# Attention in 64x64 tiles with an instruction order planned at build time

## The chip, the cores and the metric

The kernel runs on one core of one Trainium2 chip. The metric is the device time of one execution in microseconds. An execution counts as slow when it is more than 1.5% above the fastest of the same kernel; ratios compare fast ones only. The span of a profile (first to last instruction) is some 1.7 us shorter than the time of the same execution.

## The reference

```python
# q, k, v: 8 batches x 12 heads x 448 tokens x 64
scores = (q @ k.T) / sqrt(64)
attn   = maximum(scores, 0) ** 2 / 448
x      = attn @ v                                  # to 8 x 448 x 768
h      = maximum(x.T @ w_tok1, 0) @ w_tok2         # token mixing, 448 -> 256 -> 448
u      = x + h.T
out    = u + maximum(u @ w_ch1, 0) @ w_ch2         # channel mixing, 768 -> 1536 -> 768
```

Inputs and output are float32; the kernel computes in bf16 and accumulates in float32.

## The kernel before

It takes two heads a step, 48 steps. 448 keys are cut into three blocks of 128 and a remainder of 64; the remainders of the two heads share one block whose other halves are zero (`kz`, `vz`).

```python
def transposes(s):            # 16 transposes, 128x64 tiles, into one bank
    blocks = [(c * QP, QP, q_raw[:, :, c, :]) for c in range(QC)]            # 4 of 112
    blocks += [(KO + c * 128, 128, k_raw[:, :, c, :]) for c in range(KB)]    # 3 of 128
    blocks.append((KO + KM, 128, kz...))                                     # remainder
    for at, n, src in blocks:
        for h in range(2):
            nc.tensor.matmul(ps[64 * h : 64 * (h + 1), at : at + n], lhsT=src[:, h, :],
                             rhs=ident[:n, :n], is_transpose=True, ...)
    nc.vector.tensor_copy(sb, ps[:, : KO + KM + 128])

def scores(s, blocks):        # 64x128 tiles: one row half for each head
    for c in blocks:
        ps = ps_att.tile([128, 2, 512], FP32, tag="att", name="sc_ps")       # two banks
        for e in range(2):
            nc.tensor.matmul(ps[:, e, :S], lhsT=sb[h, KO + c * 128 : ...], rhs=sb[h, :S], ...)
    # ACT: at = relu(ps), both banks at once; DVE later: sq = at * at

def values(s):                # 128x64 tiles, then values_rest with a full 128x128 tile
    ...
# ... cut: x_back, token1, token2, channel1, channel2

for s in range(NS + 4):       # a fixed order, written by hand
    scores(s, (0, 1)); load_pair(s + PRE); transposes(s + 1)
    values(s - 1); scores(s, (2,)); values_rest(s - 1)
    square(); fill(0.25)      # a quarter of the step's share of channel work
    scores_rest(s); x_back(s - 2); fill(0.25); square()
    token2(...); fill(0.25); token1(...); fill(0.25)
```

Conditions and arguments are cut here. PSUM is split for good: two tiles of two banks for scores, one bank for values, three for all else. Channel work of a batch can start only when its six pairs have gone through token mixing.

## Time and profile before

| | before |
|---|---|
| median time | 413.28 us (4 runs, 411.98 to 415.08) |
| profiled span | 411.6 us |
| TensorE busy | 388.3 us, 94% |
| ACT, DVE busy | 51%, 53% |
| first channel matmul | 58.2 us |
| idle stretches of TensorE after that | hardly any until the end |

The page's busy share says which engine to look at; it does not say what a step costs, because TensorE's matmuls overlap. The distance from the start of one block to the start of the next does. The timeline of TensorE shows, in brackets, how long it stood idle and what ended that; these two rows are from the start of the kernel before:

```profile
27.76 1.86 PE L290 MATMUL t_ps<-x_sb,wt 128*128 128x256 bf16 x8 [4.38 <-DVE x_sb L280]
...
40.40 1.03 PE L290 MATMUL t_ps<-x_sb,wt 128*128 128x256 bf16 x8 [2.24 <-DVE x_sb L280]
```

Token 1 stands in the order ahead of score groups that could have run, so all of TensorE waits for one copy. The first row's eight matmuls take 1.86 us where the second's take 1.03: after 4.38 us of idling the granted clock is 0.50 there (stretch from 27.7 to 29.6 us).

### The profile page before, as it was taken

How to read it: one execution, taken by the hardware profiler on the slowest of the kernel's cores; microseconds unless marked ns; L12 is line 12 of the kernel's file. 1: busy time of each engine (PE TensorE's matmuls, PEld its weight loads, DVE VectorE, ACT ScalarE, POOL GpSimd, SP SyncE). 2: the span in 40 equal slices, each digit the busy share in tenths (PEclk: the TensorE clock that was granted, in tenths of full speed). 3: DMA queues.
4: the chain of work that ended last, by engine and by line, in shares of the span. 5: the costliest groups of instructions: out<-in, count | busy, mean ns of one | idle time of the engine just before them, and what ended most of it. 6: DMA issues, size and time to landing. Idle time of an engine off the chain costs nothing.

```text
span 411.6 us, 7596 instructions
## 1 busy us (share of the span) xinstructions
PE 388.3 (94%) x3033; PEld 205.4 (50%) x3033; DVE 216.2 (53%) x414; ACT 209.5 (51%) x313; POOL 130.8 (32%) x196
## 2 busy tenths in 40 slices
PE   5856799999999999999999999999999999999995
PEld 2323345555445555555445555555545555555562
DVE  2667774466465566365455665356444755432021
ACT  2745676743674446753575347654566237611400
POOL 8995456244243333243223424235222000000000
PEclk9778999999999999999999999999999999999999
DMA  7999999459946999469955989569953434113323
GB/s 75 119 145 203 187 180 196 57 80 126 167 50 69 137 137 143 45 93 134 134 70 56 146 131 147 57 75 134 149 70 47 93 92 92 24 47 99 60 62 93
DMA packets 101572, 43.44 MB, mean 106 GB/s; under 512 B 83424, under 2 KB 97952, under 8 KB 101536
## 3 DMA queue, kind: packets, MB, share of 16 engines
q0 software_dynamic: 54432, 21.70, 50.2%
q1 hardware_dynamic: 47104, 21.25, 25.3%
q8 instruction: 24, 0.39, 0.4%
q14 instruction: 12, 0.10, 0.1%
HBM read 43.38 MB, written 11.01 MB: 132 GB/s over the span
## 4 chain that ended last, share of the span: by engine, by line
PE 85%; DVE 7%; POOL 4%; issue 1%; DMA 1%; ACT 0%; DVEq 0%; ACTq 0%; POOLq 0%
PE m_ps L345 26%; PE m_ps L363 26%; PE sc_ps L195 8%; PE acc_ps L226 6%; PE qkT_ps L163 6%; PE t_ps L290 5%; PE h_ps L308 3%; PE acc_ps L240 3%; DVE sq L185 3%; PE sr_ps L209 2%; DVE uT_sb L316 1%; DMA wt_nat<-in_moe_w_tok_dram 1%; DVE xT L248 1%; POOL k_raw L86 1%; POOL v_raw L94 1%
## 5 line engine op out<-in xcount | busy, mean ns | idle before, releaser
L179 ACT ACTIVATE at<-sc_ps 128x896 bf16<-128x896 f32 x144 | 122.5, 922 | 60.3 <-PE sc_ps L195 59.9
L345 PE MATMUL m_ps<-uT_sb,wc 128*128 128x448 bf16 x576 | 120.3, 352 | 0.6 <-DVE uT_sb L316 0.5
L363 PE MATMUL m_ps<-wc,r_sb 128*128 128x384 bf16 x672 | 116.7, 326 | 0.0
L185 DVE TENSOR_TENSOR sq<-at 128x896 bf16<-128x896 bf16 x192 | 97.7, 559 | 0.1
L94 POOL DMA_DIRECT2D v_raw<-in_v_dram x48 | 34.5, 719 | 170.1 <-PE sc_ps L195 159.3
L363 PEld LDWEIGHTS <-r_sb 128*128 128x128 bf16 x672 | 65.6, 98 | 44.3 <-issue 0.6
L352 ACT ACTIVATE r_sb<-m_ps 128x448 bf16<-128x448 f32 x96 | 52.1, 543 | 65.9 <-PE m_ps L345 65.9
L345 PEld LDWEIGHTS <-wc 128*128 128x128 bf16 x576 | 56.2, 98 | 49.7 <-issue 1.4
L173 DVE COPY qkT<-qkT_ps 128x960 bf16<-128x960 bf16 x48 | 31.5, 656 | 85.6 <-PE qkT_ps L163 85.6
L371 DVE TENSOR_TENSOR out_sb<-m_ps,u_sb 128x384 f32<-128x384 f32 x56 | 31.1, 555 | 71.4 <-PE m_ps L363 69.2
L195 PE MATMUL sc_ps<-qkT 64*128 64x448 bf16 x288 | 45.6, 365 | 2.5 <-ACT at L179 1.3
L248 DVE TENSOR_SCALAR xT<-acc_ps 128x448 bf16<-128x448 f32 x48 | 29.9, 624 | 29.7 <-PE acc_ps L240 29.7
L226 PE MATMUL acc_ps<-sq,v_raw 128*64 128x448 bf16 x288 | 36.7, 363 | 0.0
L82 POOL DMA_DIRECT2D q_raw<-in_q_dram x48 | 33.0, 688 | 10.8 <-DMA wc<-in_moe_w_ch_dram 9.8
L86 POOL DMA_DIRECT2D k_raw<-in_k_dram x48 | 35.2, 732 | 1.7 <-DMA wc<-in_moe_w_ch_dram 1.7
L179 ACT ACTIVATE at<-sr_ps 128x448 bf16<-128x448 f32 x48 | 26.2, 545 | 16.8 <-PE sr_ps L209 16.8
L290 PE MATMUL t_ps<-x_sb,wt 128*128 128x256 bf16 x192 | 25.7, 278 | 9.0 <-DVE x_sb L280 9.0
L298 ACT ACTIVATE r_sb<-t_ps 128x512 bf16<-128x512 f32 x24 | 14.3, 597 | 38.4 <-PE t_ps L290 38.4
L195 PEld LDWEIGHTS <-qkT 64*128 64x128 bf16 x288 | 10.8, 94 | 37.2 <-issue 35.8
L316 DVE TENSOR_TENSOR uT_sb<-h_ps,xT 128x448 bf16<-128x448 f32 x48 | 27.6, 615 | 2.0 <-PE h_ps L308 2.0
L290 PEld LDWEIGHTS <-wt 128*128 128x128 bf16 x192 | 19.0, 99 | 15.0 <-issue 5.1
L163 PEld LDWEIGHTS <-q_raw 112*64 112x64 bf16 x384 | 12.3, 113 | 22.4 <-issue 18.0
(36 smaller groups left out, 209.0 us busy)
## 6 DMA issues: line engine op xcount, KB each, us to landing
q_raw<-in_q_dram POOLq DMA_DIRECT2D x48, 112.0 KB, 3.9
k_raw<-in_k_dram POOLq DMA_DIRECT2D x48, 96.0 KB, 4.2
v_raw<-in_v_dram POOLq DMA_DIRECT2D x48, 96.0 KB, 2.9
out_dram<-out_sb SPq DMA_DIRECT2D x8, 336.0 KB, 2.8
wc<-in_moe_w_ch_dram POOLq DMA_DIRECT2D x2, 1152.0 KB, 12.0
wc<-in_moe_w_ch_dram POOLq DMA_DIRECT2D x4, 576.0 KB, 9.0
out_dram<-out_sb SPq DMA_DIRECT2D x8, 288.0 KB, 2.7
out_dram<-out_sb SPq DMA_DIRECT2D x8, 240.0 KB, 2.8
```

What stands on the lines that cost most here:

```text
L86: nc.gpsimd.dma_start(out=k_raw.rearrange("p h c d -> p h (c d)"), in_=k[b, h0 : h0 + 2, :KM].rearrange("h (p c) d -> p h (c d)", c=KB),)
L94: nc.gpsimd.dma_start(out=v_raw.rearrange("p h c d -> p h (c d)"), in_=v[b, h0 : h0 + 2, :KM].rearrange("h (p c) d -> p h (c d)", c=KB),)
L163: nc.tensor.matmul(ps[64 * h : 64 * (h + 1), at : at + n], lhsT=src[:, h, :], rhs=ident[:n, :n], is_transpose=True, start=True, stop=True, ...
L179: nc.scalar.activation(at, ps[:, :, :S], AF.Relu)
L185: nc.vector.tensor_tensor(out=sq, in0=at, in1=at, op=ALU.mult)
L195: nc.tensor.matmul(ps[:, e, :S], lhsT=sb[h, KO + c * 128 : KO + (c + 1) * 128], rhs=sb[h, :S], start=True, stop=True,)
L226: nc.tensor.matmul(ps[64 * e : 64 * (e + 1), :S], lhsT=v_raw[:, e, c, :], rhs=sq[:, e, :], start=(c == 0), stop=False, skip_group_check=True,)
L248: nc.vector.tensor_scalar(out=xT[b % 2][:, p, :S], in0=ps[:, :S], scalar1=float(alpha2), scalar2=None, op0=ALU.mult,)
L290: nc.tensor.matmul(ps[:, j, :], lhsT=wt1[:, c, j * 128 : (j + 1) * 128], rhs=x_sb[:, :, c, :], start=(c == 0), stop=(c == 3),)
L345: nc.tensor.matmul(ps[:, :S], lhsT=wc1[:, g, e * 128 : (e + 1) * 128], rhs=uT[:, g, off : off + S], start=(g == 0), stop=(g == CC - 1),)
L352: nc.scalar.activation(r2[:, e, off : off + S], ps[:, :S], AF.Relu)
L363: nc.tensor.matmul(ps[:, :HN], lhsT=r2[:, e, tok], rhs=wc2[:, e, cols], start=(e == 0), stop=(e == EC - 1), skip_group_check=True,)
```

## The change

Intent: use the array fully in attention, remove the remainder blocks, and let no engine stand behind something that is not ready. Four heads a step, 24 steps; seven key chunks of 64; each group of four matmuls uses the four 64x64 tiles; every PSUM tile is one of eight equal banks. A planner simulates the engines at build time from a table of durations, and emits each engine's instructions in the order that came out. That order is fixed in the program. What follows is the core of a diff that rewrites most of the file, shortened and with comments added.

```diff
-    NP = H // 2
-    KB = 3
-    KM = KB * 128
+    KC = 7
+    KP = S // KC
+    GS = H // 4
+    NS = B * GS
-        ps = ps_att.tile([128, 2, 512], FP32, tag="att", name="sc_ps")
+            o.ps = [bank(o, e, "sc_ps") for e in range(2)]
+            for half in range(2):
+                for e in range(2):
+                    rows = slice(64 * e, 64 * (e + 1))
+                    nc.tensor.matmul(
+                        o.ps[e][64 * half : 64 * (half + 1), :S],
+                        lhsT=kT[rows, c * KP : (c + 1) * KP],
+                        rhs=kT[rows, S:], ...
+            for c in range(KC):                       # values
+                for half in range(2):
+                    for e in range(2):
+                        nc.tensor.matmul(o.ps[half][64 * e : 64 * (e + 1), :S],
+                            lhsT=r[rows, e, c * D : (c + 1) * D], rhs=sq[rows, e, :], ...
+        # relu: on ACT, or on DVE when ACT is taken for more than the slack
+        durs={"ACT": 0.424, "DVE": 0.534}, slack=0.45
+        # x to token-major: on TensorE for s < 9, else a transposing transfer
+        dur=1.23, work=2.0
+    o.seen = ring[e] + 1.0 + SEM                      # planner: when a transfer has landed
+    plan.run(bursts, gap=3.3)                         # in place of the loop above
```

Loads also change: rows of 1,792 bytes, and no separate transfers for remainders.

## The prediction

> **What bounds the kernel now.** I read the page's first two parts for the engine that is always busy, then the stretches table to split the run into stages, then the timeline of one steady step to price each part by start-to-start distances, then the waits.
>
> ```profile
> PE 388.3 (94%) x3033; PEld 205.4 (50%) x3033; DVE 216.2 (53%) x414; ACT 209.5 (51%) x313; POOL 130.8 (32%) x196
> ...
> PE   5856799999999999999999999999999999999995
> ...
> PEclk9778999999999999999999999999999999999999
> ```
>
> TensorE is full except in the first six slices and the last one. The stretches say the same: 17 us of the first 58 have no matmul at all, then almost nothing is missing.
>
> ```profile
> 0.00:58.00 58.00, 40.78 (x381) 19.78 (x382) 37.04 (x78) 31.96 (x42) 43.40 (x69) 0.88 1.18 151
> ...
> 205.40:252.00 46.60, 46.60 (x377) 24.84 (x376) 26.77 (x50) 25.05 (x38) 15.10 (x22) 1.00 0.83 102
> ```
>
> Busy time overstates, because matmuls overlap: one of L195 lasts 365 ns while four start within 480. So I price by starts, in this TensorE timeline of a steady pair of heads (start, length, what, count):
>
> ```profile
> 205.38 0.55 PE L195 MATMUL sc_ps<-qkT 64*128 64x448 bf16 x4
> 205.86 0.39 PE L163 MATMUL qkT_ps<-ident,q_raw 112*64 112x112 bf16 x8
> 206.08 0.34 PE L163 MATMUL qkT_ps<-ident,k_raw 128*64 128x128 bf16 x6
> 206.25 0.22 PE L163 MATMUL qkT_ps<-ident,kz 128*64 128x128 bf16 x2
> 206.31 0.73 PE L226 MATMUL acc_ps<-sq,v_raw 128*64 128x448 bf16 x6
> 206.97 0.36 PE L195 MATMUL sc_ps<-qkT 64*128 64x448 bf16 x2
> 207.27 0.36 PE L240 MATMUL acc_ps<-sq,vz 128*128 128x448 bf16 x1
> 207.47 1.30 PE L345 MATMUL m_ps<-uT_sb,wc 128*128 128x448 bf16 x6
> 208.60 0.35 PE L209 MATMUL sr_ps<-qkT 128*128 128x448 bf16 x1
> 208.79 1.30 PE L345 MATMUL m_ps<-uT_sb,wc 128*128 128x448 bf16 x6
> 209.93 0.92 PE L308 MATMUL h_ps<-wt,r_sb 128*128 128x448 bf16 x4
> 210.72 2.43 PE L345 MATMUL m_ps<-uT_sb,wc 128*128 128x448 bf16 x12
> ```
>
> Attention of one pair: 207.47 - 205.38 = 2.09, and 0.19 for the remainder scores (208.60 to 208.79): 2.28 us. A six-matmul unit of channel 1 is 1.13 (207.47 to 208.60), two units of token 2 are 0.79 (209.93 to 210.72). By the same reading elsewhere, token 1 is 0.88, a block of four full transposes 0.22, and a twelve-matmul unit of channel 2 1.95 (the spacing of its evictions at the end). Sum: 48 x 2.28 = 109.4; 24 x 0.88 = 21.1; 24 x 0.79 = 19.0; 12 x 0.22 = 2.6; 96 x 1.13 = 108.5; 56 x 1.95 = 109.2. Together 369.8 of the span of 411.6, so 41.8 us are not matmul streaming.
>
> Where are they? The first channel matmul starts at 58.2. Until then the timeline holds about 9.7 pairs, three token blocks of each kind and seven transposes: 22.1 + 2.6 + 2.4 + 1.5 = 28.6 us of work. So **29.6 us** are lost in the start. The last matmul ends at 406.6, so **5.0** are the tail (eviction and store). The remaining **7.2** are scattered. The start is a chain through other engines, not a full engine:
>
> ```profile
> PE t_ps L290 <- DVE x_sb L280: 9.0, 4, 4.4
> ```
>
> Token 1 stands in TensorE's order before work that was ready, and waits for a transposed copy; ACT is busy 32 and DVE 37 of those 58 us.
>
> **What the Trainium skill says.**
> - "TensorEngine Tiling (Array Packing)", Key Properties: 64x64 gives four tiles that run independently, and a change of tiling mode drains the engine. The trace agrees on the drain: four scores in 64-row tiles should stream for 2 x 187 = 373 ns and take 480 to the next mode; the last two take 300 instead of 187. About 0.1 us a switch. Two tiles do run at once here; four at once no run has shown.
> - "TensorE: Matmul & The Clock Gate", Back-to-back issue gap: about N/2.4 + 2.5 ns, and not below some 25 ns a matmul however small N is. The first half agrees (1130/6 = 188 ns at 448 columns, 1950/12 = 162 at 384). The floor is not visible: the sixteen transposes take 450 ns, 28 each, but two tiles of 112 or 128 columns give 25 by streaming alone.
> - "ScalarE: Activation LUTs", What ACT_TABLE_LOAD costs: 186 ns + 0.833 ns a column, back-to-back ones overlapping by 93. The trace has 922 ns for 896 columns and 545 for 448, and two of 896 in 1.72 us, so 0.80 apart. For 448 that gives 0.80 - 448 x 0.83 = 0.43 us each (my estimate from these rows).
>
> **The change, part by part.**
> *64x64 tiles.* 448 keys become seven chunks of 64, so there is no remainder block with half-empty tiles. For four heads: scores 7 x 0.19 = 1.33 and values 7 x 0.19 = 1.33 us, each group of four matmuls streaming together. Transposes: 56 matmuls of 64 columns. Streaming alone is 14 x 64/2.4 = 0.37 us, the planner in the diff allows 0.63, and the skill's floor gives 56 x 25 = 1.4. I choose 0.75, near the planner's, because its other constants (0.189, 0.1625, 0.378) are what I read above.
> *Switches.* Counting the built order, mode changes fall from 195 to 106, 4.4 per four heads: 0.44 us. Sum for four heads 0.75 + 1.33 + 1.33 + 0.44 = 3.85, against 2 x 2.28 = 4.56. Saved: 24 x 0.71 = **17 us**, all on the bounding engine.
> *Full transposes on TensorE* (the start only): nine blocks of eight, 9 x 0.44 = 4.0 instead of 2.6: **+1.4**. Token and channel work is unchanged. New streaming sum: 92.4 + 21.1 + 19.0 + 4.0 + 108.5 + 109.2 = 354.2.
> *Order by planner.* In the built order the first channel unit stands after 28 score groups, 5 transposes, 3 values and three each of the mixing blocks: 3.8 + 5.3 + 4.0 + 6.3 + about 1 of switches = 20.4 us of TensorE work. What sets its time is now ACT, because the planner leaves 327 of 336 relus there: 56 x 0.43 = 24 plus five copies at 0.80 and six small evictions at 0.47 is 31 us, of which the last 3 need not be done; the first relu can start at about 7 to 7.5 (loads land near 5, as before). So the first channel unit is at about 35.5, and the start loses 15 us instead of 29.6: **-14.5**.
> *Single-bank PSUM.* 336 relus of 448 columns instead of 144 of 896 and 48 of 448: ACT 327 x 0.43 + 93 x 0.43 + 24 x 0.80 + 24 x 0.43 + 24 x 0.5 = 222 us in all, about 60% of the new span; DVE some 190. Neither binds on average. Gain: banks come free singly, worth part of the 7.2 scattered us; I keep 5.
> *Loads.* Rows of 1,792 bytes instead of 768 and 1,024, and 144 issues for q, k and v instead of 176 with remainders. Transfers are hidden in the steady part already, so nothing but safety there.
> Sum: 354.2 + 15.2 + 5 + 5.0 = 379.4 us of span; time exceeds span by 2.7 before (414.28 - 411.6): **382**.
>
> **The rivals.**
> 1. *Small transposes bind by issue.* At 1.4 us per four heads the gain shrinks by 24 x 0.65 = 16 us: time 398. For it: the skill's floor, and 28 ns a matmul in the trace. Against: streaming explains those 28, and the author's constant.
> 2. *ACT becomes the bound while attention runs.* A burst of three score groups leaves six relus, 2.6 us, and the planner puts at least 3.3 us of other work between bursts; with channel 1's evictions ACT is some 70 to 80% full there. If real waits are longer than planned, a fixed order lets TensorE wait for banks: 24 steps x 0.5 us is 12 us, time 394. Against: the last 69 us or so of the order are channel work alone, so attention has slack as a whole.
> 3. *Weights arrive late.* Channel 1 is now wanted 22 us earlier. Until all channel weights are in, 10 MB must land (counted in bf16), 60 us at the 150 to 200 GB/s of the start here. A stall there costs 5 to 10 us: 390.
> 4. *Everything goes to plan*: transposes 0.63, stalls 2, start 13: 372.
>
> **Range and chances.** 382 lies between the plan's own success (372) and one full rival (390 to 398); two rivals together would reach 405. I take 370 to 398. To be less than 2% faster (above 406) needs nearly all rivals at once. Faster 0.96, same 0.03, slower 0.01.
>
> **What would show each step.** Right: scores and values at 0.19 us per four starts; a transpose block of 56 near 0.75; first channel matmul near 35 us; switches near 0.1; tail 5; idle TensorE time between 60 us and the tail below 6; ACT busy (by its overlapping lengths) near 270. Wrong: transpose blocks above 1.1; four tiles that pair up (0.37 per four), which would add 24 x 2.6 = 60 us; waits of score groups on ACT in the steady part; waits of channel matmuls on weight transfers around 35 to 65 us.

## The result, and the profile after

The changed kernel took a median of 390.97 us (fast runs 390.28 to 391.0; one run of 396.58 was slow). The ratio to the kernel before is 0.9459 (95% interval 0.942 to 0.9497): 5.4% faster. Such a ratio is taken over fast runs of the same rounds, so it need not be the ratio of the medians.

The page's parts 1 and 2 of the changed kernel answer to those of before:

```profile
PE 369.5 (95%) x4305; PEld 206.2 (53%) x4305; DVE 194.6 (50%) x346; ACT 239.7 (62%) x493; POOL 93.1 (24%) x159
...
PE   6997999999999978979999999999999999999994
...
PEclk9999999999999996999999999999999999999999
```

The start is fuller. But in slices 15, 16 and 18 TensorE has gaps that the kernel before did not have, and in slice 16 the clock falls. TensorE's timeline of a steady step of four heads:

```profile
203.20 0.38 PE L418 MATMUL sc_ps<-kqT 64*64 64x448 bf16 x4
203.41 1.49 PE L469 MATMUL acc_ps<-sq,v_raw 64*64 64x448 bf16 x28
204.74 0.39 PE L380 MATMUL kqT_ps<-ident,k_raw 64*64 64x64 bf16 x28
204.95 0.46 PE L380 MATMUL kqT_ps<-ident,q_raw 64*64 64x64 bf16 x28
205.22 0.57 PE L418 MATMUL sc_ps<-kqT 64*64 64x448 bf16 x8
205.72 3.58 PE L659 MATMUL m_ps<-uT_sb,wc 128*128 128x448 bf16 x18
209.23 0.76 PE L418 MATMUL sc_ps<-kqT 64*64 64x448 bf16 x12
209.93 2.44 PE L659 MATMUL m_ps<-uT_sb,wc 128*128 128x448 bf16 x12
```

By starts: 28 values matmuls take 1.33 us (204.74 - 203.41), so four tiles do stream at once; 56 transposes take 0.48 (205.22 - 204.74; 0.49 in most blocks), under 9 ns each. Three score groups take 0.70, of which 0.13 over 3 x 0.19 is the change of mode. Now the gap:

```profile
141.34 2.44 PE L659 MATMUL m_ps<-uT_sb,wc 128*128 128x448 bf16 x12
147.54 1.89 PE L575 MATMUL t_ps<-x_sb,wt 128*128 128x256 bf16 x8 [3.75 <-DMA x_sb<-xT]
149.22 2.45 PE L659 MATMUL m_ps<-uT_sb,wc 128*128 128x448 bf16 x6
...
173.95 1.05 PE L575 MATMUL t_ps<-x_sb,wt 128*128 128x256 bf16 x8 [1.63 <-ACT sq L252]
```

Token 1 waits 3.75 us for the transfer that transposes x, while channel units that could have run stand behind it. Then the six matmuls of the third row take 2.38 us (149.22 to 151.60, where the next block starts) instead of 1.13. The stretches view of the same time (stretch, busy times, then clock, DMA share and GB/s) shows why:

```profile
146.70:153.60 6.90, 6.06 (x38) 2.99 (x42) 0.36 (x1) 2.49 (x6) 0.00 (x0) 0.51 0.15 51
```

The granted clock was 0.51 for 6.9 us. "TensorE: Matmul & The Clock Gate" of the Trainium skill, in the section on why this matters for your kernels, warns of idle gaps over some 3 us for this reason; the trace agrees, with 3.75 us of idling. The tile view of `x_sb` has how long such transfers took from issue to landing:

```profile
DMA to landing us min/median/max: 3.0/5.5/9.5
```

The one issued at 138.0 is the 9.5. The wait in the last row of the gap's timeline is of the same kind: the bracket names ACT, but the transfer of that block, issued at 166.85, landed at 173.90 by the trace, 0.05 us before token 1 started, and the waits of TensorE's weight loads have one of 2.1 us on it there. In the kernel before these transfers took 4.1 us at the median and 5.6 at most, and no wait of TensorE on one appears among its waits.

To see where the time went I add up, over all matmuls of a trace, the distance from each start to the next, and subtract a price for the work when it streams: transposes 0.45 us for 56 (a little under the 0.46 of the cleanest block) and 0.45 for the 16 of before, a score group 0.19, a values block 1.33, a channel unit 1.13 or 1.96, and so on, from the steady rows above and those in the prediction. What is left over is lost to waits, a low clock and changes of mode. The run is cut at the first channel matmul and at the last values block; the first loss includes the 1.2 us before the first matmul, and the last part is the time after the last matmul started. A price that is 0.05 us off for one block of each step moves a figure by 1.2 us (24 steps) or 2.4 us (48 steps).

| us | streaming | lost before the first channel matmul | lost while attention runs | after | span |
|---|---|---|---|---|---|
| before | 354.5 | 32.5 | 19.2 | 5.3 | 411.6 |
| changed | 336.1 | 22.5 | 25.2 | 5.5 | 389.2 |

So the change saves some 18 us of streaming and 10 in the start, and loses 6 in the middle, although it has 89 fewer mode changes there and in the start together (106 against 195).

A part of the first loss is a low clock that the page's PEclk row does not show: the first values block, at 15.86 us, takes 2.68 us instead of 1.33, with its groups of four 0.373 us apart instead of 0.189.

### The profile page after: what moved, and what is told of

Its sections match the earlier page's. It is cut to its first block, busy times and chain, and to the rows that moved or that the text cites. A ratio compares the mean times of both kernels' runs of the same rounds, so it can differ in the third digit from the quotient of the medians.

```text
span 389.2 us, 10290 instructions
## 1 busy us (share of the span) xinstructions
PE 369.5 (95%) x4305; PEld 206.2 (53%) x4305; DVE 194.6 (50%) x346; ACT 239.7 (62%) x493; POOL 93.1 (24%) x159
## 4 chain that ended last, share of the span: by engine, by line
PE 80%; ACT 8%; DMA 5%; DVE 3%; issue 1%; POOL 1%; ACTq 0%; POOLq 0%
PE m_ps L692 27%; PE m_ps L659 26%; PE sc_ps L418 8%; PE t_ps L575 6%; ACT sq L252 5%; PE acc_ps L469 5%; PE h_ps L603 5%; DMA x_sb<-xT 4%; PE kqT_ps L380 2%; ACT kqT L258 1%; DVE sq L451 1%; DMA q_raw<-in_q_dram 1%; PE x_ps L546 1%; ACT xT L494 1%; POOL k_raw L275 1%
## 5 line engine op out<-in xcount | busy, mean ns | idle before, releaser
L252 ACT ACTIVATE sq<-sc_ps 128x448 bf16<-128x448 f32 x327 | 153.9, 586 | 32.6 <-PE sc_ps L418 32.6
L451 DVE TENSOR_TENSOR sq<-sq 128x896 bf16<-128x896 bf16 x168 | 102.7, 621 | 74.3 <-ACT sq L252 73.3
L418 PE MATMUL sc_ps<-kqT 64*64 64x448 bf16 x672 | 53.7, 376 | 1.2 <-ACT kqT L258 1.0
L469 PE MATMUL acc_ps<-sq,v_raw 64*64 64x448 bf16 x672 | 38.6, 363 | 0.0
L418 PEld LDWEIGHTS <-kqT 64*64 64x64 bf16 x672 | 19.2, 108 | 25.2 <-issue 20.3
L275 POOL DMA_DIRECT2D k_raw<-in_k_dram x48 | 29.3, 628 | 10.4 <-DMA wc<-in_moe_w_ch_dram 8.9
L469 PEld LDWEIGHTS <-v_raw 64*64 64x64 bf16 x672 | 20.5, 111 | 13.8 <-issue 2.9
L258 ACT ACTIVATE kqT<-kqT_ps 128x896 bf16<-128x896 bf16 x24 | 22.6, 942 | 6.4 <-PE kqT_ps L380 6.1
L603 PE MATMUL h_ps<-wt,r_sb 128*128 128x448 bf16 x96 | 22.9, 353 | 2.8 <-ACT kqT L258 1.7
L252 ACT ACTIVATE r_sb<-t_ps 128x512 bf16<-128x512 f32 x24 | 15.2, 632 | 14.1 <-PE t_ps L575 14.1
L260 DVE COPY kqT<-kqT_ps 128x896 bf16<-128x896 bf16 x24 | 14.8, 617 | 9.8 <-PE kqT_ps L380 9.8
```

The costliest lines, as they stand in the source:

```text
L252: nc.scalar.activation(out, ps, AF.Relu)
L258: nc.scalar.activation(out, ps, AF.Copy)
L275: nc.gpsimd.dma_start(out=raws[t][s % NR][64 * half : 64 * (half + 1)], in_=src[b, h0 : h0 + 2].rearrange("e (p c) d -> p e (c d)", c=KC),)
L418: nc.tensor.matmul(o.ps[e][64 * half : 64 * (half + 1), :S], lhsT=kT[rows, c * KP : (c + 1) * KP], rhs=kT[rows, S:], start=True, stop=True ...
L451: lambda o: nc.vector.tensor_tensor(out=buf, in0=buf, in1=buf, op=ALU.mult),
L469: nc.tensor.matmul(o.ps[half][64 * e : 64 * (e + 1), :S], lhsT=r[rows, e, c * D : (c + 1) * D], rhs=sq[rows, e, :], start=(c == 0), stop=( ...
```

## The experiments

Ten kernels ran, all with correct results. Each is compared with the kernel before on the same chip in the same rounds. E1 to E4 ran on one chip, E5 to E8 on a second, E9 and E10 on a third, so comparisons across these groups go by the ratio to before. Theories: (1) the middle's loss comes from orders built on landings that came later than planned; rival, from ACT, which is busier than before (240 us against 210). (2) The start is set by ACT; rival, by a chain. (3) Tiles and planner each contribute; rival, the planner gives back in the middle what it gains in the start.

### E1: tell the planner how late the transfer lands

```diff
-                    o.seen = ring[e] + 1.0 + SEM
+                    o.seen = ring[e] + 1.0 + SEM + o.lag
@@ the transposing transfer of x
                     work=2.0,
+                    lag=5.0,
```

> The planner is told that the transfer that transposes x lands 5 us later than it assumed (the profile has 5.5 us median and 9.5 at worst from issue to landing; the planner allows about 5.5 only for an empty queue and the one issued at 138.0 landed at 147.5). Nothing else is changed; the built order now keeps channel units ahead of each token-1 block that waits for such a transfer. Theory A (the 3.75 us hole at 143.8 and the half clock after it, together 6.9 us, come from an order built on too short a landing): the hole is gone, the clock stays 1.0 after the start, time 384 (382 to 386). Rival B (the transfer is late because the queues are full and something else then waits instead): 388 to 391.

Measured: **381.28 us** (380.83 to 381.76), ratio 0.9215, faster than expected. No instruction is added or dropped from the math; only the order differs, plus six relus that the planner moved to DVE. TensorE's timeline where the gap was:

```profile
144.42 0.57 PE L418 MATMUL sc_ps<-kqT 64*64 64x448 bf16 x8
144.82 1.49 PE L469 MATMUL acc_ps<-sq,v_raw 64*64 64x448 bf16 x28
146.15 0.39 PE L380 MATMUL kqT_ps<-ident,k_raw 64*64 64x64 bf16 x28
146.36 0.46 PE L380 MATMUL kqT_ps<-ident,q_raw 64*64 64x64 bf16 x28
146.63 0.61 PE L418 MATMUL sc_ps<-kqT 64*64 64x448 bf16 x8
147.19 1.04 PE L576 MATMUL t_ps<-x_sb,wt 128*128 128x256 bf16 x8
148.06 2.43 PE L660 MATMUL m_ps<-uT_sb,wc 128*128 128x448 bf16 x12
```

Token 1 now follows a whole burst of attention, and its transfer is there. The transfers themselves are no quicker (median 5.1, longest 11.8 us). The loss in the middle falls from 25.2 to 16.2 us: 6.9 of it around the old gap and about 2 at the wait at 172 us.

### E2 and E3: share the relus between ACT and DVE

```diff
-                    slack=0.45,
+                    slack=0.1,
```

> The slack after which DVE may take a relu from ACT goes from 0.45 to 0.1 us; the built order gives DVE 101 of 336 relus instead of 9. Theory A (the start is bound by ACT: busy 29.8 of the first 40.2 us, some 90% from its first relu on): first channel matmul near 36 instead of 40.3, and fewer short waits on ACT in the steady part; time 385 (383 to 388), with the hole at 143 left as it is or moved. Rival B (the start is a chain of latencies, not ACT's load): first channel matmul at 39 to 41, time 389 to 392.

> Both of the edits before. If both theories hold and do not overlap: 379 (376 to 382). If the relus only cure the start: 385. If neither: 390.

Measured: E2 394.76 us (ratio 0.9523; one of its four executions was slow), E3 382.14 (0.9236). Both are misses. The first channel matmul came at 42.2 and 41.0 us, not at 36. The stretch before it, in E2 (order of the busy times: TensorE, its weight loads, DVE, ACT, GpSimd):

```profile
0.00:42.20 42.20, 33.89 (x549) 17.24 (x549) 29.90 (x58) 26.86 (x54) 27.48 (x49) 0.92 1.11 159
```

ACT fell from 29.8 to 26.9 us and DVE rose from 25.4 to 29.9: the load moved across, and the last values block of the batch ended 1.7 us earlier (32.9 instead of 34.6). But from there to the first channel matmul it took 9.3 us instead of 5.6 (8.3 in E3). Part of that is the clock: from 34 to 43 us it was 0.62 in E2 and 0.81 in E3, and the eight token-1 matmuls took 1.87 us instead of 1.03. In E2 it fell at 34.3 us, although no wait of TensorE since 30 us had been longer than 0.8 us. So neither run tests a lighter ACT at full clock; E9 does. E2 also had new waits of token 1 on x transfers in the middle (7.3 us over six waits); E3, with late landings planned for, had none, which is E1's point again.

### E4: the tiles without the planner

All operations stay as changed; TensorE's order is written as before, banks are taken in turn, relus stay on ACT.

```diff
-    plan.run(bursts, gap=3.3)
+    for s in range(NS + 2):
+        go(S[s, 0]); go(S[s, 1]); go(S[s, 2]); go(T[s + 1]); go(V[s - 1]); feed(s + 3)
+        go(S[s, 3]); square(); fill(0.25)
+        go(S[s, 4]); go(S[s, 5]); go(S[s, 6]); go(X[s - 1]); fill(0.25); square()
+        go(t2[s - 2]); fill(0.25); go(t1[s - 1]); fill(0.25)
```

(Names and conditions are shortened here.)

> The 64x64 tiles, the loads and the single banks of the changed kernel, but its planner off: TensorE's order is that of the kernel before (three score groups, transposes, values, one score group, a quarter of the channel share, three score groups and so on), banks in turn, relus all on ACT, squares where they stood. From the measured costs (transposes 0.45, scores 0.19 a group, values 1.33, 86 switches of 0.1) streaming is 345 us. Theory A (the planner's gain in the start is given back in the middle): start loss 30, tail 5, scattered 7, time 389 to 392, so the same as the changed kernel. Rival B (the planner is worth its 14 us): 400 to 405.

Measured: **403.38 us**, ratio 0.9752. Rival B is right: against this order by hand the planner is worth some 12 us (0.9752 against 0.9459), even with its late transfers. Its table row: streaming 336.1, start 34.0, middle 25.6, after 5.3. So streaming falls by the same 18.4 us, the start is no better than before, and the middle is 6.4 worse than in the kernel before: in this order channel units wait for DVE's last sums of a batch (4.9 us over eight waits). In its start TensorE waits 6.5 us for loads of q and k (1.0 in the changed kernel), so how much of the 12 us is TensorE's order and how much later loads is not separated.

### E5: four tiles, but neighbours use only two of them

From E1; the planner is told the longer block too.

```diff
-            for c in range(KC):
-                sq = sqs[(s * KC + c) % NSQ]
-                for half in range(2):
+            for half in range(2):
+                for c in range(KC):
+                    sq = sqs[(s * KC + c) % NSQ]
```

> From E1 (381.3): the values loop runs over the two halves of the rows outside and the seven chunks inside, so that neighbours in TensorE's order are only two column tiles of the same rows; the planner is told 7 x 0.378. Same matmuls, same results. Theory A (four 64x64 tiles stream together, but only when the four stand next to each other in the order): a values block takes 2.65 instead of 1.33 us, 24 x 1.32 = 32 us longer, time 411 to 415. Rival B (the array finds the free tiles itself, whatever the order): 381 to 384.

Measured: 395.9 us (ratio 0.9598, against 0.9215 for E1): by the ratios some 16 us slower than E1, between the theories. The timeline of one values block and the transposes that follow it in the order:

```profile
206.99 1.52 PE L469 MATMUL acc_ps<-sq,v_raw 64*64 64x448 bf16 x22
208.31 0.20 PE L380 MATMUL kqT_ps<-ident,k_raw 64*64 64x64 bf16 x2
208.35 0.35 PE L469 MATMUL acc_ps<-sq,v_raw 64*64 64x448 bf16 x2
208.36 0.22 PE L380 MATMUL kqT_ps<-ident,k_raw 64*64 64x64 bf16 x2
208.54 0.35 PE L469 MATMUL acc_ps<-sq,v_raw 64*64 64x448 bf16 x2
208.55 0.22 PE L380 MATMUL kqT_ps<-ident,k_raw 64*64 64x64 bf16 x2
208.73 0.35 PE L469 MATMUL acc_ps<-sq,v_raw 64*64 64x448 bf16 x2
```

The array looks ahead a little. In this block a second pair of matmuls joins 0.58 us after the start, as the fourth of the first half's seven chunks begins, and transposes that stand behind all 28 values matmuls start before the last of them. Values and transposes together take 2.37 us (206.99 to 209.36, where the next scores start) instead of 1.81: 24 x 0.56 = 13 us, which is most of the difference. The planner's order changed with the longer block, and what the rest is was not tested. So the order within a block matters, but a tile is not idle until its turn comes.

### E6 and E7: split the banks for good

From E1. The split is not quite that of the kernel before, whatever the expectation says: three two-bank tiles for transposes, scores and values, and two banks for all else, where before had two such tiles for scores, one bank for values and three for all else, transposes among them.

```diff
+                    if c.shape == "s":        # transposes, scores, values
+                        return any(max(banks[k : k + 2]) <= at for k in (0, 2, 4))
+                    return min(banks[6:]) <= at
@@ E7 only: one relu for both banks of a score group
-                    lambda o, e=e: relu(o, buf[:, e], u.ps[e][:, :S]),
+                    lambda o, e=e: relu(o, buf, u.pair[:, :, :S]),
```

> From E1: the eight banks are split as in the kernel before, six in three two-bank tiles for transposes, scores and values, two for everything else; every half is still evicted by its own instruction. The planner then needs 148 mode switches instead of 106. Theory A (the free pool of eight single banks is what lets long bursts run): 42 more switches of some 0.12 us and short waits for the two remaining banks, time 386 to 393. Rival B (the split does not matter): 380 to 383.

> As the run with split banks, but the two banks of a score group are relu'd by one ACT instruction of 896 columns, as before the change (150 switches). ACT saves about 168 x 0.06 = 10 us in all. If ACT's load matters: 4 us or more faster than the split alone. If ACT is off the path: within 2 us of it.

Measured: E6 391.5 us (0.9476), E7 390.35 (0.9447). Against E1's 0.9215 this split costs 2.6% of the time before, some 11 us: 42 fewer mode changes and a free choice of bank are worth that much against it. What the old split would cost was not run. The first channel matmul is 3.9 us later (43.7 instead of 39.8), most of the rest is in the middle. Evicting two banks at once, as before the change, gains some 0.3%. So the shared pool pays, and the size of the eviction hardly matters.

### E8: no transposing transfers for x

```diff
-    XDMA = 9
+    XDMA = 24
```

> The changed kernel (391.0, planner not told of late landings) with all 24 x blocks transposed on TensorE and copied by DVE: no token-1 block waits for a transfer. Adds 15 x 0.44 = 6.6 us of TensorE and 15 x 0.55 us of DVE. Theory A (all of E1's 9.7 us came from late x transposes): the gaps go, 391.0 - 9.7 + 6.6 = 388 (386 to 390), clock 1.0 in the middle. Rival B (E1's new order gained by something else): 395 to 398.

Measured: **388.24 us**, ratio 0.9395, as theory A has it. In the profile the clock was 0.999 and the middle lost 16.0 us, the same as in E1, with 6.6 us more to stream. Two independent ways of not waiting for x transfers recover the same 9 us, so the cause is settled. That they land late because each step's six loads share the transfer engines with them is likely (the DMA share was 1.26 and 1.40 in the two parts of the longest one's 9.5 us, and 0.66 in the 4 us before) but no run took the loads away.

### E9: a middle setting of the slack

E1 with the slack at 0.4 us.

> E1 with the relu slack at 0.4 us: 70 relus on DVE, between E1's 15 and E3's 102. If the start is bound by ACT and DVE together (busy 29.8 and 25.4 of 40.2 us) and only the balance was wrong in E2 and E3: first channel matmul 38 to 39, time 379 to 381. If the start is a chain whose order counts more than the balance: 381 to 383, no gain.

Measured: 380.56 us, ratio 0.922, first channel matmul at 39.5 us. No difference from E1 that counts (0.9215). The clock was 1.00 from 34 to 43 us here. The last values block ended at 32.2 us (34.2 in E1), and the chain after it took 7.3 us (5.6 in E1; 0.7 of the 7.3 are waits for q loads): most of what the lighter ACT gained was lost again after it.

### E10: denser attention

```diff
-    plan.run(bursts, gap=3.3)
+    plan.run(bursts, gap=2.6)
```

> E1 with the minimum of other work between attention bursts cut from 3.3 to 2.6 us, so attention runs denser (about 10.5 instead of 11.5 us per four heads) and the channel-only end grows. Mode switches stay 106. Rival 2 of the prediction (ACT nearly binds while attention runs: some 9.7 us of ACT per four heads): TensorE waits for relus, 385 or more. If ACT has room: 380 to 383.

Measured: 381.82 us, ratio 0.9242. In the stretch from 60 to 250 us, E10 first, then E1:

```profile
60.00:250.00 190.00, 187.04 (x2823) 106.44 (x2822) 136.44 (x244) 166.27 (x350) 58.44 (x99) 1.00 0.88 130
```

```profile
60.00:250.00 190.00, 187.63 (x2677) 108.12 (x2676) 127.41 (x225) 146.18 (x307) 56.79 (x96) 1.00 0.84 129
```

ACT goes from 77% to 88% busy and TensorE stays at 98%: ACT does not bind the middle at either setting.

## Why the prediction was right or wrong

The time of 391.0 lies in the predicted range, 9 us above the predicted 382. E1 lands at 381.3, but not because every step held: two errors of the sum happen to cancel once the late transfers are gone.

- **Tiles: right, and the transposes were better than chosen.** Scores and values cost 0.19 a group as worked out. The transpose block was put at 0.75 us; it is 0.49 in most blocks and 0.46 in the cleanest. Over 24 steps that is some 6 to 7 us to the good. Rival 1 (an issue floor near 1.4 us) is refuted by the trace.
- **Switches: slightly low.** 0.11 to 0.13 us each in the timeline, where 0.1 was taken: 106 x 0.02 = 2 us.
- **Start: 4.8 us later than put.** The first channel matmul was put at 35.5 us and came at 40.3 (58.2 before). The step that failed is "what sets its time is now ACT". ACT is indeed almost without gaps from its first relu to 35.3, but that relu came at 9.2 us, not 7 to 7.5, since the last q rows landed near 7. And after the last values block of the batch a chain follows that no filling of ACT shortens. ACT's timeline, and below it TensorE's, at the end of the start:

```profile
34.54 0.73 ACT L494 ACTIVATE xT<-acc_ps 128x448 bf16<-128x448 f32 x1
37.90 0.60 ACT L252 ACTIVATE r_sb<-t_ps 128x512 bf16<-128x512 f32 x1 [2.63 <-PE t_ps L575]
```

```profile
35.32 0.67 PE L546 MATMUL x_ps<-ident,xT 128*128 128x128 bf16 x8 [0.68 <-ACT xT L494]
36.77 1.03 PE L575 MATMUL t_ps<-x_sb,wt 128*128 128x256 bf16 x8 [0.78 <-DVE x_sb L260]
...
38.55 0.93 PE L603 MATMUL h_ps<-wt,r_sb 128*128 128x448 bf16 x4
...
40.26 3.56 PE L659 MATMUL m_ps<-uT_sb,wc 128*128 128x448 bf16 x18
```

  From 35.3 to 40.3 each step waits for the one before it: transposes, copy, token 1, relu, token 2, sum. These 5.0 us were not in the sum. With the 2 at the beginning, and less the 2 by which ACT's stretch was shorter than put (26.1 us instead of 28), they make about the 4.8. The loss of the table is 22.5 against 15.2 predicted, 7.3 more, because the prediction counted about 1 us of switches and 1.5 more of transposes as work. E9 shows at full clock that a lighter ACT alone gains little: the chain after it grew by most of what was won. No run shortened the chain itself.
- **Scattered losses: the term that was mis-sized.** The step that failed is "Transfers are hidden in the steady part already". The sum kept 5 us, beside 10.6 of switches. Measured are 25.2 in the middle, switches included. 9.0 of them are token-1 blocks that stood in a fixed order behind transfers landing later than planned, with the halved clock that followed (E1, E8); without them it is 16.2, about the 15.6 of the sum. None of the four rivals named these transfers. Rival 3 had the right kind of cause on the wrong transfer: no wait of TensorE on a channel weight appears in the profile.
- **Rival 2 (ACT binds) was not it:** E10. ACT's predicted 270 us of busy time are 240.
- **Single banks:** predicted as worth a part of 7 us; against E6's split it is some 11, against the old one it was not run. **Tail:** predicted 5.0 from the last matmul's end, measured 5.2 (5.5 from its start, as in the table).

Put together, by the prices of the table: 7.2 less for transposes, 7.3 more in the start, some 9.6 more for switches and scatter, 0.5 in the tail make 10, and the span is 389.2 where 379.4 was predicted. Time above span was 1.7 us where 2.7 was taken, since the prediction set the median of several runs against one profiled run.

## What to carry to other kernels

An order fixed at build time turns any transfer that lands later than assumed into idling of everything behind it, so plan with the worst landing under load and not with that of an empty queue; five microseconds of extra allowance for one kind of transfer gave some 10 us here (0.9215 against 0.9459) without a new instruction. Let all users draw from one pool of single PSUM banks when the order is planned, and put matmuls of different array tiles next to each other. When a start is the loss, follow the serial chain to the first work of the busiest engine before shifting load between its helpers, and look at the granted clock there before judging the result.

## What the Trainium skill lacked or had wrong

- "TensorE: Matmul & The Clock Gate", What overlaps and what doesn't (in its part on row and column tiling): it says that matmuls keep program order in start and end. In E5, transposes that stand behind all 28 values matmuls started at 208.31 us, and values matmuls at 208.35, 208.54 and 208.73. Ends are modelled in this profile, so nothing is said of them.
- The same page, Back-to-back issue gap: the floor of about 25 ns a matmul is given without a word on tiles, and does not hold across them. 56 transposes of 64 columns took 0.48 us, under 9 ns each. Within one tile it is not contradicted: the first groups of four start at 204.735, 204.763 and 204.795. The starts of one group of four stand 3 to 4 ns apart in the trace, which is what the page's own part on packing small matmuls says.
- "TensorEngine Tiling (Array Packing)", Key Properties: a change of mode drains the array, but no cost is given. Here it is 0.11 to 0.13 us each.
- None of the pages gives the latency of a transposing transfer beside loads: 3.0 us at least, 5.5 at the median and 9.5 at most here, and 11.8 in E1.
